# Attention with bucket masks, then two mixing layers: the score scale moves into the key split and the unmatched rows are mended behind the exponential

## The chip, the cores and the metric

One core of one Trainium2 chip runs the whole program. The metric is device time in microseconds (us). The kernel before took 697.1 us as the median of three runs (696.8 to 697.82).

## The reference, cut to what matters

For each of 2 x 8 heads, with 768 positions of 64 values, a row of scores may only see the keys whose bucket (six sign bits of a projection) is its own:

```python
scores = scale * np.matmul(q, k.transpose(0, 1, 3, 2))        # scale = 1/8
scores = np.where(mask, scores, -1000000000.0)
scores = scores - np.max(scores, axis=-1, keepdims=True)
attn = np.exp(scores)
attn = attn / (np.sum(attn, axis=-1, keepdims=True) + 1e-09)
return np.matmul(attn, v).astype(np.float32)
```

A row that matches no key has -1e9 everywhere, so its attention is even, 1/768 for each key. The result goes through a layer with cosines, sines and a token mixing, and then through a layer norm and an MLP of width 2048, each with residuals.

## The kernel before, in words

float32 accuracy is reached with pairs of fp32r tiles: each operand is split into a high part (`split_hi`, a cast on ScalarE, ACT) and a low part (`split_lo`, raw value minus high part, on VectorE, DVE, or GpSimd, POOL). The mask is added inside the score matmul: extra rows of bits lower an unmatched score by multiples of 2^34, so that an unmatched entry is hugely negative.

The attention works through 48 periods p. A period takes two tiles, a and b, of 128 rows by 768 keys. Its operations are named in the plans (L405 to L425): `Sa`/`Sb` score matmuls on TensorE (PE) into one PSUM tile each (one buffer per letter), `Ma`/`Mb` the negated row maximum on DVE (`s_max`, L288), `ta`/`tb` two operations on 128x1 on POOL (`s_tiny`, L292 and L293), `Ea`/`Eb` the exponential on ACT with its row sum (`s_exp`, L300), `R1` the sum plus 1e-9 (`s_guard`: DVE for p below 3, L308, POOL for the other 45, L310), `R2` the reciprocal on DVE (`s_recip`, L314), `na`/`nb` the normalization on POOL (`s_norm`, L318), `U0..U2` transposes on PE (L331), `H0..H2` their high parts on ACT (L340), `L0..L2` their low parts on DVE (L101), `PV` the product with v on PE (L356), `O` on ACT and `X` on DVE its evacuation (L365, L372).

In `s_tiny`, POOL makes two things from the negated maximum m: the scale, 0.125 if m is under 2^33 and 0 if not, and the bias, m times that scale. A row without a match so gets exp(0) = 1 everywhere, and its sum is 768.

The order on each engine in the attention is written out by hand: a step k goes through a plan and emits each operation for period k minus its lag. `plan_s` is for the first four steps, `plan_b` where bits of the later heads are computed, `plan` for the rest. `G`, `C` and `D` are places for background work: splits of q, k and v for later heads, the conversion of the theta weights (DVE: L121 and L124 in `D`, between `R1` and `R2`). In the plan, POOL's order in a step is `nb`, `G`, `R1`, `ta`, `na`, `C`, `tb`; DVE's is `Ma`, `X`, `D`, `R2`, `Mb`, `L0`, `L1`, `L2`. Engines work in the order of their own queue, so an operation that waits holds up what is behind it. Before step 1, PE runs 38 spare transposes (`warm`, L441). The last three steps and all that follows (the mixing layers) are put in order by a planner, not by hand.

The low parts of k are made on DVE for the head pairs 0, 2 and 3, and on POOL for pair 1 (whole, 128x768) and for pairs 4 to 7 (in two halves of 128x384 each).

Of the kernel before, what the change touches and what calls it, by code (L numbers as in the profile page):

```python
# [9 lines left out]
F32 = mybir.dt.float32  # L10
F32R = mybir.dt.float32r
U32 = mybir.dt.uint32
AF = mybir.ActivationFunctionType
ALU = mybir.AluOpType
AX = mybir.AxisListType
# [11 lines left out]
MISS = 2.0 ** 34  # L27
# [6 lines left out]
def attn_moe_kernel(  # L34
# [17 lines left out]
    B, H, D, S = qT.shape  # L52
# [11 lines left out]
    def f(ap):  # L64
        return ap.bitcast(F32)
# [26 lines left out]
    def cast(eng, o, i):  # L92
        if eng is act:
            act.activation(o, i, AF.Copy)  # L94
        elif eng is vec:
            vec.tensor_copy(o, i)
        else:
            pool.tensor_scalar(out=o, in0=i, scalar1=1.0, scalar2=0.0, op0=ALU.mult, op1=ALU.add)

    def sub(eng, o, i, hi):  # L100
        eng.tensor_tensor(out=o, in0=i, in1=f(hi), op=ALU.subtract)  # L101
# [64 lines left out]
    def split_hi(nm, n, eng, part=None):  # L166
        if part in (None, 0):
            hl[nm, n, 0] = bp.tile([128, S], F32R, tag=f"hi{nm}{n % NP}", name=f"hi{nm}{n}")
        r = part_of(S, part)
        cast(eng, hl[nm, n, 0][:, r], raw[nm, n][:, r])  # L170

    def split_lo(nm, n, eng, part=None):
        if part in (None, 0):
            hl[nm, n, 1] = bp.tile([128, S], F32R, tag=f"lo{nm}{n % NP}", name=f"lo{nm}{n}")
        r = part_of(S, part)
        sub(eng, hl[nm, n, 1][:, r], raw[nm, n][:, r], hl[nm, n, 0][:, r])

    vv_t = {}

# [104 lines left out]
        s_ps[p, i] = ps  # L284

    def s_max(p, i):
        m = ap_.tile([128, 3], F32, tag="m", bufs=4, name=f"m{p}_{i}")
        vec.tensor_reduce(out=m[:, 0:1], in_=s_ps[p, i][:, :, 0:HALF], axis=AX.XY, op=ALU.max, negate=True)  # L288
        m_t[p, i] = m
    def s_tiny(p, i):  # L290
        m = m_t[p, i]
        pool.tensor_scalar(out=m[:, 1:2], in0=m[:, 0:1], scalar1=MISS / 2, scalar2=0.125, op0=ALU.is_lt, op1=ALU.mult)  # L292
        pool.tensor_tensor(out=m[:, 2:3], in0=m[:, 0:1], in1=m[:, 1:2], op=ALU.mult)  # L293

    def s_exp(p, i):
        ps, m = s_ps.pop((p, i)), m_t.pop((p, i))
        if i == 0:
            l_t[p] = ap_.tile([128, 2, 2], F32, tag="l", bufs=4, name=f"l{p}")
        pt = ap_.tile([128, 2, HALF], F32, tag=f"p{i}", bufs=2, name=f"p{p}_{i}")
        act.activation(  # L300
            pt, ps[:, :, 0:HALF], AF.Exp, bias=m[:, 2:3], scale=m[:, 1:2], accum_out=l_t[p][:, 0, i:i + 1]
        )
        p_t[p, i] = pt

    def s_guard(p):
        l = l_t[p]
        if p < 3:
            vec.tensor_scalar(out=l[:, 0, :], in0=l[:, 0, :], scalar1=1e-9, scalar2=None, op0=ALU.add)  # L308
        else:
            pool.tensor_scalar(out=l[:, 0, :], in0=l[:, 0, :], scalar1=1e-9, scalar2=0.0, op0=ALU.add, op1=ALU.add)  # L310

    def s_recip(p):
        l = l_t[p]
# [2 lines left out]
    def s_norm(p, i):  # L316
        pn = ap_.tile([128, NI, 128], F32, tag=f"pn{i}", bufs=2, name=f"pn{p}_{i}")
        pool.tensor_scalar(  # L318
            out=pn.rearrange("p c s -> p (c s)"), in0=p_t.pop((p, i)).rearrange("p c s -> p (c s)"),
            scalar1=l_t[p][:, 1, i:i + 1], scalar2=0.0, op0=ALU.mult, op1=ALU.add,  # L320
        )
        pn_t[p, i] = pn

# [285 lines left out]
    def run_bg(q):  # L609
# [5 lines left out]
    ops = {  # L615
        "Sa": lambda p: s_mm(p, 0), "Sb": lambda p: s_mm(p, 1),
        "Ma": lambda p: s_max(p, 0), "Mb": lambda p: s_max(p, 1),
        "ta": lambda p: s_tiny(p, 0), "tb": lambda p: s_tiny(p, 1),
        "Ea": lambda p: s_exp(p, 0), "Eb": lambda p: s_exp(p, 1),
        "R1": s_guard, "R2": s_recip, "na": lambda p: s_norm(p, 0), "nb": lambda p: s_norm(p, 1),  # L620
        "B1": lambda p: bits_chunk(*bq[p], "T1"), "B2": lambda p: bits_y_(*bq[p]),
# [447 lines left out]
```

## Time and profile before

| what | before |
|---|---|
| runs, median of three | 697.1 us |
| profiled execution, its span from first to last instruction | 694.3 us |
| PE busy over the span | 680.1 us (98%) |
| DVE busy | 479.2 us (69%) |
| ACT busy | 386.9 us (56%) |
| POOL busy | 297.7 us (43%) |

The page of the profile gives no other time of the profiled execution than its span; the median of the runs lies 2.8 us above it. A busy PE is one with a matmul in flight, which says nothing of how closely the matmuls follow each other. The attention takes the first 240 us or so, and there all five engines are busy; in the rest of the span PE alone is.

### The profile page before, as it was taken

The page shows a single profiled execution, that of the slowest core. Times are in us where ns is not written, and L with a number is a line of the kernel's source. Part 1 is how long each engine was busy: PE and PEld are TensorE (multiplying, and loading weights), DVE is VectorE, ACT ScalarE, POOL GpSimd, SP SyncE. Part 2 cuts the span into 40 slices and gives each one's busy share as a digit, 9 for nine tenths or more (in the row PEclk, how much of TensorE's full clock was granted, in tenths as well). Part 3 has the DMA queues.
Part 4 walks back from the last instruction along what each step waited for, and adds up shares of the span by engine and source line. Part 5 has one row for each costly group of instructions (what it writes and reads, how often), then busy time and mean ns, then how long its engine had stood idle before and what let it go on. Part 6 is the DMA issues. An engine that isn't in the chain of part 4 may idle for free.

```text
span 694.3 us, 10787 instructions
## 1 busy us (share of the span) xinstructions
PE 680.1 (98%) x3694; PEld 583.3 (84%) x3694; DVE 479.2 (69%) x815; ACT 386.9 (56%) x757; POOL 297.7 (43%) x534
## 2 busy tenths in 40 slices
PE   9899999999999989999999999999999999999997
PEld 7799999999899868877888888888888888888885
DVE  6799998999999998897698789433655741121212
ACT  6799998999999976675454455211424421111110
POOL 5888889787878843334367613200121200000000
PEclk9999999999999999999999999999999999999999
DMA  8695554375552231111363335100112200010101
GB/s 256 155 200 157 145 119 107 92 166 139 124 134 77 77 91 46 47 45 46 96 185 100 121 111 190 63 1 1 62 60 79 105 1 0 1 61 0 61 0 61
DMA packets 30394, 62.17 MB, mean 90 GB/s; under 512 B 4274, under 2 KB 11058, under 8 KB 30340
## 3 DMA queue, kind: packets, MB, share of 16 engines
q1 hardware_dynamic: 30340, 61.48, 31.6%
q8 instruction: 30, 0.49, 0.3%
q14 instruction: 24, 0.20, 0.1%
HBM read 39.98 MB, written 3.15 MB: 62 GB/s over the span
## 4 chain that ended last, share of the span: by engine, by line
PE 53%; DVE 20%; ACT 10%; POOL 7%; issue 6%; DMA 2%; SPq 1%; POOLq 0%; ACTq 0%; DVEq 0%
PE h L947 19%; PE oc L966 19%; DVE m L288 3%; DVE ptl L101 3%; ACT p L300 3%; PE s L280 3%; PE o L356 3%; PE a L798 3%; PE t L331 3%; DVE cs L121 2%; ACT pth L340 2%; DVE cy L124 2%; PE acc L757 2%; DVE z L101 2%; POOL pn L318 2%
## 5 line engine op out<-in xcount | busy, mean ns | idle before, releaser
L117 POOL TENSOR_SCALAR cs<-st 128x256 f32<-128x256 f32 (+2 forms) x78 | 52.1, 672 | 154.3 <-DVE cy L124 84.5
L950 ACT ACTIVATE hh<-h 128x512 fp32r<-128x512 f32 x48 | 28.5, 596 | 143.7 <-PE h L947 109.6
L300 ACT ACTIVATE p<-s,m 128x768 f32<-128x768 f32 x96 | 95.5, 995 | 7.2 <-POOL m L293 5.6
L951 DVE SCALAR_TENSOR_TENSOR hl<-h,hh 128x512 fp32r<-128x512 f32 x48 | 32.8, 685 | 93.8 <-ACT hh L950 93.8
L288 DVE TENSOR_REDUCE m<-s 128x1 f32<-128x768 f32 x96 | 90.8, 947 | 8.0 <-PE s L280 4.1
L757 PE MATMUL acc<-z,tokh 128*128 128x512 f32 x288 | 91.2, 395 | 1.1 <-ACT z L94 0.4
L318 POOL TENSOR_SCALAR pn<-p,l 128x768 f32<-128x768 f32 x96 | 87.5, 912 | 10.7 <-DVE l L314 8.7
L101 DVE TENSOR_TENSOR ptl<-t,pth 128x512 fp32r<-128x512 f32 x144 | 91.1, 680 | 0.3 <-ACT pth L340 0.2
L280 PE MATMUL s<-tk,tq 128*128 128x384 f32 (+1 forms) x360 | 82.1, 350 | 2.1 <-ACT p L300 1.9
L331 PE MATMUL t<-ident,pn 128*128 128x128 f32 x576 | 81.1, 274 | 1.7 <-POOL pn L318 1.2
L340 ACT ACTIVATE pth<-t 128x512 fp32r<-128x512 f32 x144 | 81.1, 595 | 1.5 <-PE t L331 0.2
L331 PEld LDWEIGHTS t<-ident,pn 128*128 128x128 f32 x576 | 67.7, 140 | 9.2 <-POOL pn L318 1.7
L966 PE MATMUL oc<-w2h,hh 128*128 128x512 f32 x192 | 75.0, 391 | 0.3 <-ACT hh L950 0.2
L966 PE MATMUL oc<-w2l,hh 128*128 128x512 f32 x192 | 74.9, 390 | 0.0
L966 PE MATMUL oc<-w2h,hl 128*128 128x512 f32 x192 | 74.7, 391 | 0.0
L757 PEld LDWEIGHTS acc<-z,tokh 128*128 128x128 f32 x288 | 53.3, 188 | 13.2 <-DVE z L101 1.3
L280 PEld LDWEIGHTS s<-tk,tq 128*128 128x128 f32 (+1 forms) x360 | 58.5, 189 | 6.9 <-ACT p L300 6.6
L114 ACT ACTIVATE cy<-st 128x256 f32<-128x256 f32 (+2 forms) x78 | 42.7, 552 | 31.2 <-DVE w2l L101 8.4
L121 DVE SCALAR_TENSOR_TENSOR cs<-st,cs 128x256 uint32<-128x256 uint32 (+2 forms) x78 | 54.3, 699 | 5.9 <-POOL cs L117 5.7
L757 PE MATMUL acc<-z,tokl 128*128 128x512 f32 x144 | 55.5, 391 | 0.0
L124 DVE SCALAR_TENSOR_TENSOR cy<-cy,cs 128x256 uint32<-128x256 uint32 (+2 forms) x78 | 48.3, 627 | 3.0 <-ACT cy L114 2.2
L356 PE MATMUL o<-pth,vv 128*128 128x256 f32 x288 | 46.5, 296 | 0.2 <-POOL vv L101 0.2
(174 smaller groups left out, 1402.7 us busy)
## 6 DMA issues: line engine op xcount, KB each, us to landing
st<-in_w_dram SPq DMA_DIRECT2D x26, 512.0 KB
tq<-hiq SPq DMA_DIRECT2D x30, 192.0 KB
tk<-hik SPq DMA_DIRECT2D x30, 192.0 KB
st<-in_wrT_dram SPq DMA_DIRECT2D x12, 384.0 KB
st<-in_wiT_dram SPq DMA_DIRECT2D x12, 384.0 KB
vs<-in_v_dram SPq DMA_DIRECT2D x8, 384.0 KB
st<-in_w_dram SPq DMA_DIRECT2D x12, 256.0 KB
out_dram<-U SPq DMA_DIRECT2D x12, 256.0 KB
```

The costliest lines, as they stand in the source:

```text
L101: eng.tensor_tensor(out=o, in0=i, in1=f(hi), op=ALU.subtract)
L121: vec.scalar_tensor_tensor(out=su, in0=t[:, :, 0], scalar=29, in1=su, op0=ALU.logical_shift_right, op1=ALU.bitwise_or)
L280: pe.matmul(ps[:, hf, 0:HALF], lt[0:K, x * 128:(x + 1) * 128], rt[0:K, hf * HALF:(hf + 1) * HALF], start=(K == 128), stop=(K != 128),)
L288: vec.tensor_reduce(out=m[:, 0:1], in_=s_ps[p, i][:, :, 0:HALF], axis=AX.XY, op=ALU.max, negate=True)
L300: act.activation(pt, ps[:, :, 0:HALF], AF.Exp, bias=m[:, 2:3], scale=m[:, 1:2], accum_out=l_t[p][:, 0, i:i + 1])
L318: pool.tensor_scalar(out=pn.rearrange("p c s -> p (c s)"), in0=p_t.pop((p, i)).rearrange("p c s -> p (c s)"), scalar1=l_t[p][:, 1, i:i + 1 ...
L331: pe.transpose(ps[:, w * 128:(w + 1) * 128], pn_t[p, i][:, c, :], ident)
L340: act.activation(ph, t_ps[p, u], AF.Copy)
L356: pe.matmul(ps, vv[:, c, e].rearrange("p a d -> p (a d)"), x[:, c::NI, :], start=(k == 0), stop=(k == 2 * NI - 1),)
L757: pe.matmul(acc, w[:, x, t * 128:(t + 1) * 128], z[:, x, y, :], start=(j == 0 and k == 0), stop=(j == NI - 1 and k == 5),)
L947: pe.matmul(ps, w[:, d, x * 128:(x + 1) * 128], XN[k][y][:, d, :], start=(n == 0), stop=(n == 11))
L966: pe.matmul(acc2[t], lt[:, t * 128:(t + 1) * 128], w[:, x, :], start=(first and n == 0), stop=(last and n == 2),)
```

## The change

k is multiplied by 1/8 at its split: the high part by the scale of the cast; the low part on DVE in one operation with two inputs (k times 0.125 minus the high part), on POOL by an extra operation in place on the raw tile before the subtraction. The exponential then takes the negated maximum itself as bias and no scale, so `s_tiny` goes. In its place `s_lone` runs once a period at the place of `tb`, on 128x2 for both tiles: two POOL operations that give 1/768 and 1e30 where m is at least 2^33 (no match), else 0. `R1` adds 1e-9 and the second of these to the sum, now on DVE for every period, and `s_norm` adds the first to the normalized row. A row without a match so gets something divided by about 1e30, plus 1/768. The tile m is one of 128x3x2 for each period where it was one of 128x3 for each letter; four buffers both times.

```diff
-        cast(eng, hl[nm, n, 0][:, r], raw[nm, n][:, r])
+        eng.activation(hl[nm, n, 0][:, r], raw[nm, n][:, r], AF.Copy, scale=0.125 if nm == "k" else 1.0)
...
-        sub(eng, hl[nm, n, 1][:, r], raw[nm, n][:, r], hl[nm, n, 0][:, r])
+        hi, lo = (hl[nm, n, y][:, r] for y in range(2))
+        x = raw[nm, n][:, r]
+        if nm == "q":
+            sub(eng, lo, x, hi)
+        elif eng is vec:
+            vec.scalar_tensor_tensor(out=lo, in0=x, scalar=0.125, in1=f(hi), op0=ALU.mult, op1=ALU.subtract)
+        else:
+            pool.tensor_scalar(out=x, in0=x, scalar1=0.125, scalar2=0.0, op0=ALU.mult, op1=ALU.add)
+            sub(pool, lo, x, hi)
...
     def s_max(p, i):
-        m = ap_.tile([128, 3], F32, tag="m", bufs=4, name=f"m{p}_{i}")
-        vec.tensor_reduce(out=m[:, 0:1], in_=s_ps[p, i][:, :, 0:HALF], axis=AX.XY, op=ALU.max, negate=True)
-        m_t[p, i] = m
-    def s_tiny(p, i):
-        m = m_t[p, i]
-        pool.tensor_scalar(out=m[:, 1:2], in0=m[:, 0:1], scalar1=MISS / 2, scalar2=0.125, op0=ALU.is_lt, op1=ALU.mult)
-        pool.tensor_tensor(out=m[:, 2:3], in0=m[:, 0:1], in1=m[:, 1:2], op=ALU.mult)
+        if i == 0:
+            m_t[p] = ap_.tile([128, 3, 2], F32, tag="m", bufs=4, name=f"m{p}")
+        vec.tensor_reduce(
+            out=m_t[p][:, 0, i:i + 1], in_=s_ps[p, i][:, :, 0:HALF], axis=AX.XY, op=ALU.max, negate=True
+        )
+
+    def s_lone(p):
+
+        m = m_t[p]
+        for x, c in ((1, 1.0 / S), (2, 1e30)):
+            pool.tensor_scalar(
+                out=m[:, x, :], in0=m[:, 0, :], scalar1=MISS / 2, scalar2=c, op0=ALU.is_ge, op1=ALU.mult
+            )
...
-            pt, ps[:, :, 0:HALF], AF.Exp, bias=m[:, 2:3], scale=m[:, 1:2], accum_out=l_t[p][:, 0, i:i + 1]
+            pt, ps[:, :, 0:HALF], AF.Exp, bias=m[:, 0, i:i + 1], accum_out=l_t[p][:, 0, i:i + 1]
...
     def s_guard(p):
         l = l_t[p]
-        if p < 3:
-            vec.tensor_scalar(out=l[:, 0, :], in0=l[:, 0, :], scalar1=1e-9, scalar2=None, op0=ALU.add)
-        else:
-            pool.tensor_scalar(out=l[:, 0, :], in0=l[:, 0, :], scalar1=1e-9, scalar2=0.0, op0=ALU.add, op1=ALU.add)
+        vec.scalar_tensor_tensor(
+            out=l[:, 0, :], in0=l[:, 0, :], scalar=1e-9, in1=m_t[p][:, 2, :], op0=ALU.add, op1=ALU.add
+        )
...
-            scalar1=l_t[p][:, 1, i:i + 1], scalar2=0.0, op0=ALU.mult, op1=ALU.add,
+            scalar1=l_t[p][:, 1, i:i + 1], scalar2=m_t[p][:, 1, i:i + 1], op0=ALU.mult, op1=ALU.add,
...
-        "ta": lambda p: s_tiny(p, 0), "tb": lambda p: s_tiny(p, 1),
+        "ta": lambda p: None, "tb": s_lone,
```

## Rows read from the trace of the kernel before

**Rows 1.** Busy time by engine in windows: start:end, length, then engines, granted clock.

```profile
40.00:80.00 40.00, 39.61 (x297) 37.70 (x296) 38.02 (x65) 39.10 (x82) 36.25 (x75) 1.00 0.61 148
...
200.00:240.00 40.00, 39.50 (x283) 36.07 (x281) 38.93 (x72) 38.88 (x81) 31.86 (x69) 1.00 0.26 85
240.00:280.00 40.00, 36.87 (x188) 30.21 (x187) 37.42 (x62) 29.52 (x55) 17.18 (x19) 1.00 0.23 68
...
440.00:480.00 40.00, 40.00 (x192) 33.06 (x191) 13.76 (x23) 7.59 (x13) 2.72 (x4) 1.00 0.00 0
```

**Rows 2.** Waits by engine, steady attention (40 to 250 us): total, times, longest.

```profile
PEld s L280 <- ACT p L300: 6.3, 20, 0.7
...
ACT p L300 <- POOL m L293: 1.4, 3, 0.7
```

**Rows 3.** Groups of instructions, shapes apart: count, busy and mean, idle before.

```profile
L318 POOL TENSOR_SCALAR pn<-p,l 128x768 f32<-128x768 f32 x96 | 87.5, 912 | 10.7 <-DVE l L314 8.7 <-PE t L331 0.7 <-PE s L280 0.3
...
L292 POOL TENSOR_SCALAR m<-m 128x1 f32<-128x1 f32 x96 | 23.8, 248 | 12.9 <-DVE m L288 7.8 <-DVE l L308 1.9
...
L293 POOL TENSOR_TENSOR m<-m 128x1 f32<-128x1 f32 x96 | 19.1, 199 | 7.9
...
L310 POOL TENSOR_SCALAR l<-l 128x2 f32<-128x2 f32 x45 | 11.0, 243 | 7.4 <-ACT p L300 4.5
```

**Rows 4.** Timeline of DVE, 17 us: the guard and reciprocal of period 0.

```profile
17.45 0.16 DVE L308 TENSOR_SCALAR l<-l 128x2 f32<-128x2 f32 x1
17.65 0.17 DVE L314 RECIPROCAL l<-l 128x2 f32<-128x2 f32 x1
```

**Rows 5.** Timeline of all engines, 10 to 20 us: start, duration, instruction.

```profile
10.01 1.81 POOL L101 TENSOR_TENSOR lok<-rawk,hik 128x768 fp32r<-128x768 f32 x1
10.02 2.03 DVE L101 TENSOR_TENSOR pb_hi<-pbr,pb_hi 128x192 fp32r<-128x192 f32 x1 [0.20 <-ACT pb_hi L94]
...
10.52 4.37 PE L441 MATMUL warm<-ident 128*128 128x128 f32 x38
...
15.55 0.65 POOL L467 TENSOR_SCALAR bits<-bb,cst_sb 64x384 fp32r<-64x384 f32 x1
...
15.60 0.99 ACT L300 ACTIVATE p<-s,m 128x768 f32<-128x768 f32 x1 [0.96 <-POOL m L293]
...
15.93 0.61 PE L459 MATMUL s<-bk,bits 7*128 7x384 f32 x2
...
16.73 0.62 PE L451 MATMUL s<-tkz,hiq 128*128 128x384 f32 x2 [0.19 <-ACT p L300]
```

**Rows 6.** Timeline of ACT and PE, 29 to 30 us.

```profile
29.07 0.99 ACT L300 ACTIVATE p<-s,m 128x768 f32<-128x768 f32 x1 [2.22 <-POOL m L293]
...
29.97 0.44 PE L331 MATMUL t<-ident,pn 128*128 128x128 f32 x2 [1.22 <-POOL pn L318]
```

**Rows 7.** Timeline of POOL, DVE and ACT, 138 to 140 us.

```profile
137.99 0.73 POOL L101 TENSOR_TENSOR thl<-cy,thh 128x256 fp32r<-128x256 f32 x1
...
138.18 0.42 DVE L372 TENSOR_TENSOR xT<-o,ot 64x256 f32<-64x256 f32 x1
...
139.08 0.17 DVE L314 RECIPROCAL l<-l 128x2 f32<-128x2 f32 x1 [0.48 <-POOL l L310]
...
139.67 0.99 ACT L300 ACTIVATE p<-s,m 128x768 f32<-128x768 f32 x1 [0.69 <-POOL m L293]
```

**Rows 8.** Busy time over one cycle of six periods, 160.58 to 187.38 us.

```profile
sum 26.80, PE 26.43 PEld 24.52 DVE 25.79 ACT 26.17 POOL 21.18; mean PE 8.81 PEld 8.17 DVE 8.60 ACT 8.72 POOL 7.06
```

**Rows 9.** Timeline of that cycle's turn, 182 to 188 us.

```profile
182.78 0.24 POOL L310 TENSOR_SCALAR l<-l 128x2 f32<-128x2 f32 x1
...
187.38 0.42 DVE L372 TENSOR_TENSOR xT<-o,ot 64x256 f32<-64x256 f32 x1 [0.57 <-ACT ot L365]
```

**Rows 10.** Timeline of the last period's b, 232 to 236 us.

```profile
232.44 0.93 DVE L288 TENSOR_REDUCE m<-s 128x1 f32<-128x768 f32 x1
...
236.04 1.03 ACT L300 ACTIVATE p<-s,m 128x768 f32<-128x768 f32 x1
```

More of the change, by code (lines that the diff above doesn't have):

```diff
@@ L286, in s_max @@
     def s_max(p, i):
-        m = ap_.tile([128, 3], F32, tag="m", bufs=4, name=f"m{p}_{i}")
-        vec.tensor_reduce(out=m[:, 0:1], in_=s_ps[p, i][:, :, 0:HALF], axis=AX.XY, op=ALU.max, negate=True)
-        m_t[p, i] = m
-    def s_tiny(p, i):
-        m = m_t[p, i]
-        pool.tensor_scalar(out=m[:, 1:2], in0=m[:, 0:1], scalar1=MISS / 2, scalar2=0.125, op0=ALU.is_lt, op1=ALU.mult)
-        pool.tensor_tensor(out=m[:, 2:3], in0=m[:, 0:1], in1=m[:, 1:2], op=ALU.mult)
+        if i == 0:
[9 more added lines that the diff above has]
+            )
     def s_exp(p, i):
-        ps, m = s_ps.pop((p, i)), m_t.pop((p, i))
+        ps, m = s_ps.pop((p, i)), m_t[p]
         if i == 0:
```

## The prediction, made before the changed kernel ran

> **What bounds the kernel now.** I read the busy times by window first. From 440 us on PE is busy 40.00 of 40 us and the other engines mostly idle; in 40 to 80 and 200 to 240 us PE, DVE and ACT are each busy over 38 of 40 [rows 1]. So the late part can't gain, and whatever the attention wins or loses reaches the end one for one, since PE has no slack behind it in which to lose it again. The change touches only the attention (the first 240 us) and what leaves it.
>
> Then the waits. In the steady attention the two small POOL operations hold the exponential up for 1.4 us in all, three times, and PE's score matmuls wait 6.3 us for an exponential to free their PSUM tile [rows 2]. So the delay that the change removes is mostly hidden: the exponential comes when ACT's own queue lets it. The timelines show where it isn't hidden: the first four steps [rows 5, 6], one place at 139 us [rows 7], and the drain of the last period [rows 10]. Last I read the stretch with the theta conversions, which repeats a cycle of six periods in 26.80 us: DVE is busy 25.79, ACT 26.17, PE 26.43 of it [rows 8]. What is to be seen there is that no engine has much room, DVE 1.01 us per cycle.
>
> **The change, part by part.** POOL loses 96 times 248 and 199 ns and 45 times 243 ns, 23.8 + 19.1 + 11.0 = 53.9 us [rows 3]. It gains two operations per period on 128x2, 96 in all; the nearest are the 243 and 248 ns of the same rows, so about 23.8 us. The scaling of k on POOL adds one 128x768 operation and eight of half that size: 912 ns for a whole one [rows 3], a half between 456 and 912, so 4.6 to 8.2 us. POOL is relieved by 53.9 - 23.8 - 4.6 (or 8.2) = 22 to 25.5 us; it is the engine with the most idle time in the attention (31.86 of 40 busy [rows 1]), so this counts only through waits. Behind each added scaling wait the subtraction and then `na`; its cover is POOL's idle time, and without it each would delay the transposes by its 0.5 to 0.9 us. Scaling in the cast adds no instruction to ACT; the low part of k on DVE keeps its two inputs and its size, so I cost both at nothing, at most 0.05 us for each DVE split, at a time when DVE waits for PE anyway.
>
> DVE gains 45 guards. When guard and reciprocal stood on DVE before, they started at 17.45 and 17.65: 0.20 us, since the second needs the first [rows 4]. That is the price with `R2` right behind; with a conversion between them it is between nothing and 0.20, I take 0.10. In a theta cycle four guards are of the first kind and two of the second: 4 x 0.20 + 2 x 0.10 = 1.0 us, as much as DVE's whole idle time there, 26.80 - 25.79 = 1.01 [rows 8]. Over the cycle's long DVE part the lag builds up, and behind it come `Mb`, the exponential and the low parts. It meets 0.57 us in which `X` waits for ACT [rows 9] and some 0.4 in smaller pieces. On the other side the exponential starts some 0.5 us sooner after the maximum (248 + 199 ns and the steps between), so DVE may be that much later without ACT noticing, and ACT's own idle time is 0.63 us per cycle. The bounds for the cycle are +1.0 (nothing is absorbed) and -0.37 (PE's idle time, 26.80 - 26.43, is the most that can be won). I take 0, for the 3.5 cycles of that stretch too; their bounds are +3.5 and -1.3. In the rest of the steady attention, as from 40 to 80 us, DVE is idle 40 - 38.02 = 1.98 us [rows 1], over some nine periods (4.4 us each) about 0.2 us per period, which is the guard's price; I take 0 there as well.
>
> The start. Exponential b of period 0 waited 0.96 us for POOL, and the scores of period 1 that need its PSUM tile left PE idle 0.19 us [rows 5]. PE's spare transposes run from 10.52 to 14.89, so nothing before that can help. Between 0.19 (what PE shows) and 0.96 (the whole wait) I take 0.4, two such waits, one for each letter. At 29.07 the exponential waited 2.22 us for POOL, but PE's next stop, 1.22 us, is for a normalized tile [rows 6], behind which POOL does as many operations as before; I take 0, bounds 0 and -1.2. At 10.01 a low part of k on POOL and a small split on DVE start together; DVE's took 2.03, to the end of POOL's 1.81 [rows 5]. The scaling now stands ahead of that subtraction: the DVE split either slips in between (sooner, covered by the spare transposes) or ends behind both (up to 0.9 later, 0.4 after what the exponential gains). I take 0, bound +0.4.
>
> At 139 us the reciprocal waited 0.48 for a guard that stood behind POOL's conversion, and the exponential 0.69 [rows 7]. The guard on DVE goes right behind `X`, from 138.60; with 0.20 the reciprocal starts at 138.80 and not at 139.08: -0.3, bounds 0 and -0.7.
>
> The drain. The last maximum ended at 233.37, its exponential started at 236.04 [rows 10], 2.67 us later, as POOL had two normalizations (2 x 0.9 us) and weight conversions ahead of `tb`. ACT could be there some 1.8 us sooner, but DVE is busy 37.42 of 40 us right behind and PE loses only 40 - 36.87 = 3.1 us there [rows 1]. A third of 1.8: -0.6, bounds 0 and -1.8.
>
> Sum: -0.4 - 0.3 - 0.6 = -1.3 us. On the profiled execution 694.3 becomes 693.0; the median lies 2.8 above the span, so 695.8. 0.2% is 1.4 us, about what a measurement of this kernel can tell from no change.
>
> **The rivals.**
>
> *DVE becomes the bound of the theta stretch (slower).* If of the 1.01 us only the 0.57 at `X` can be used, and all six guards cost 0.20, the cycle grows by 1.2 - 0.57 = 0.63, and 3.5 cycles by 2.2: with the gains elsewhere 695.8 + 2.2 = 698.0; with nothing absorbed 699.3. It decides against the gains from 1.3 / 3.5 = 0.37 per cycle, that is from a guard of (0.57 + 0.37) / 6 = 0.16 us. For it speaks that DVE is full there; against it that each period's later maximum has half a microsecond of new room before ACT misses it. A second way to a dear guard: at 10.02 a DVE operation with both inputs in SBUF stood still until POOL's was over [rows 5], and the new guard also reads two SBUF tiles. But POOL's guard started at 182.78, so by then POOL was through with its background work, and its next long operation waits for the reciprocal: the port is mostly free when DVE's guard comes. The Trainium skill (SBUF — State Buffer, Who interferes with whom) states this as a lock: a DVE instruction with two SBUF inputs and a GpSimd one that reads SBUF exclude each other, the later is blocked for the whole instruction, while a DVE instruction with at most one SBUF input, outside the two-port modes, is free of it. The trace agrees at 10.02; by that rule a guard that meets a normalization waits up to 912 ns where the old one-input form would not, and 45 half waits would be some 20 us, an upper estimate that the order of the queues excludes.
>
> *The waits pay in full (faster).* The start gives 0.96 and the 1.22 of PE, 139 us gives 0.69, with the drain's 0.6: 3.5 us, 693.6. For it: POOL's relief moves everything that stands behind it. Against it: PE's queue is in order and at the start holds bit matmuls and transposes that wait for POOL's same number of operations.
>
> *The planner orders the drain and the mixing otherwise.* It sees other durations on POOL and DVE. PE loses 3.1 us in 240 to 280; half of that either way is 694.3 or 697.4, with the other terms.
>
> *Letter a waits for b.* The maxima of both letters now lie in one tile; were waits kept by whole tiles, `Ea` would wait for `Mb`. The trace excludes it: at 15.93 PE read one half of the bits tile while POOL wrote the other until 16.20 [rows 5].
>
> **How the numbers follow.** The forecast (a small gain, 694.7 to 696.8) gets 0.50, about half of it over 0.2%: faster 0.26, same 0.24. DVE as bound 0.24: slower 0.18, same 0.06. Full waits 0.18, all faster. The planner 0.08: 0.03, 0.02, 0.03. Faster 0.47, same 0.32, slower 0.21. The range reaches into both rivals, from 693.2, below the full waits, to 698.8, between the DVE rival's two times.
>
> **What would show it.** Right: the exponential's waits for POOL gone; the reciprocal at most 0.2 us behind the guard on DVE; a theta cycle of 26.6 to 27.0 us; the stop of 0.48 at 139 us gone; the last exponential at its maximum's end. Wrong: cycles of 27.2 us and more with DVE without idle time, guards on DVE longer than 0.2 us while POOL is busy, or another order of work behind 234 us that moves PE's idle time there.

## The result and the profile after

The changed kernel takes 703.35 us (median of four runs, 702.47 to 704.25) against 697.33 for the kernel before, measured beside it: a ratio of 1.0087, 95% interval 1.0073 to 1.0101. It is 6 us slower, where a small gain was forecast. The profiled span grew from 694.3 to 700.7 us, and by where the time lies the 6.4 us split into parts. The marks are the starts of letter a's maximum in period 4 (the steady attention begins), in period 46 (the drain begins), and the last `xT`; each was read in the timeline of DVE.

| stretch | before | after |
|---|---|---|
| start to the maximum of period 4 | 35.51 | 35.16 |
| periods 4 to 46 | 190.95 | 194.37 |
| maximum of period 46 to the last `xT` | 31.00 | 33.20 |
| last `xT` to the end | 436.9 | 438.0 |

The attention loses 3.4 us and the part behind it 3.3. The windows of the changed kernel (columns as in [rows 1]) show both:

```profile
40.00:80.00 40.00, 39.11 (x293) 36.47 (x290) 39.44 (x73) 37.40 (x80) 32.25 (x49) 1.00 0.58 144
200.00:240.00 40.00, 39.03 (x291) 35.95 (x289) 39.50 (x80) 37.59 (x82) 27.89 (x45) 1.00 0.26 85
240.00:280.00 40.00, 34.76 (x177) 28.13 (x178) 37.53 (x60) 28.35 (x54) 19.26 (x21) 1.00 0.23 69
440.00:480.00 40.00, 40.00 (x189) 33.06 (x189) 17.29 (x34) 7.98 (x14) 4.72 (x7) 1.00 0.09 30
```

POOL and ACT are less busy from 40 to 80 us than in [rows 1], yet PE is too, and DVE has gone from 38.02 to 39.44 of 40 (an instruction that stands still counts as busy): the bound has moved to DVE. From 240 to 280 PE is busy 34.76 in place of 36.87.

The groups of the changed operations (count, busy, mean ns, idle before), to be held against [rows 3]:

```profile
L332 POOL TENSOR_SCALAR pn<-p,l,m 128x768 f32<-128x768 f32 x96 | 95.7, 998 | 49.1 <-DVE l L328 28.6 <-ACT p L315 8.4 <-PE t L345 5.8
...
L315 ACT ACTIVATE p<-s,m 128x768 f32<-128x768 f32 x96 | 86.8, 905 | 1.5 <-DVE m L298 0.5 <-DVE l L322 0.5
...
L306 POOL TENSOR_SCALAR m<-m 128x2 f32<-128x2 f32 x96 | 23.7, 247 | 5.9 <-DVE m L298 0.6
...
L322 DVE SCALAR_TENSOR_TENSOR l<-l,m 128x2 f32<-128x2 f32 x48 | 15.2, 317 | 0.7
...
L184 POOL TENSOR_SCALAR rawk<-rawk 128x384 f32<-128x384 f32 x8 | 4.1, 514 | 0.6
```

The line that stands out is the guard on DVE: 128x2 like the 0.16 us of [rows 4], but 317 ns on average, where its neighbour, the reciprocal, takes 162. A mean of twice the shortest says that some instructions are far longer. The timeline of DVE and POOL around one of them:

```profile
84.57 0.51 POOL L184 TENSOR_SCALAR rawk<-rawk 128x384 f32<-128x384 f32 x1
85.17 1.00 POOL L101 TENSOR_TENSOR lok<-rawk,hik 128x384 fp32r<-128x384 f32 x1
85.19 0.42 DVE L386 TENSOR_TENSOR xT<-o,ot 64x256 f32<-64x256 f32 x1
85.64 0.55 DVE L322 SCALAR_TENSOR_TENSOR l<-l,m 128x2 f32<-128x2 f32 x1
86.22 0.17 DVE L328 RECIPROCAL l<-l 128x2 f32<-128x2 f32 x1
86.31 0.94 DVE L298 TENSOR_REDUCE m<-s 128x1 f32<-128x768 f32 x1
86.57 0.99 POOL L332 TENSOR_SCALAR pn<-p,l,m 128x768 f32<-128x768 f32 x1 [0.40 <-DVE l L328]
```

The guard starts at 85.64, nothing is ahead of it, and it ends at 86.19, just behind the end of POOL's subtraction (85.17 + 1.00 = 86.17). Fifteen of the 48 guards took 0.33 to 0.92 us, twelve of them to the end of a subtraction that POOL was in, three to that of another POOL operation; the others took 0.14 to 0.18. The twelve that were held in periods 5 to 25 stand 6.8 us longer in all than 0.15 each would. In the kernel before, the subtraction of this step was over well before `X` ended, so that a guard behind `X` would have met nothing:

```profile
83.18 1.01 POOL L101 TENSOR_TENSOR lok<-rawk,hik 128x384 fp32r<-128x384 f32 x1
84.51 0.42 DVE L372 TENSOR_TENSOR xT<-o,ot 64x256 f32<-64x256 f32 x1
```

There the subtraction starts 1.33 us ahead of `X`, in the changed kernel 0.02. POOL, done at 86.17, then waits another 0.40 for the reciprocal that had to come behind the guard. The view of waits from 40 to 250 us shows who is late (total, times, longest):

```profile
POOL pn L332 <- DVE l L328: 26.0, 30, 2.3
PEld t L345 <- POOL pn L332: 10.8, 27, 0.6
ACT pth L354 <- PE t L345: 9.2, 26, 0.7
...
ACT p L315 <- DVE m L298: 0.5, 2, 0.3
```

The exponential's waits for POOL [rows 2] are gone as forecast; in their place POOL waits for DVE (8.7 us, 15 times before), the transposes for POOL, and ACT for the transposes (0.2 us before). These totals are not the loss: with the guard as a reduction (below), where the attention is faster than in the kernel before, the first three are still 21.1, 7.6 and 6.2 us.

In the drain PE's stops are other ones than before. Its timeline (the bracket is the idle time before and what ended it):

```profile
246.77 0.98 PE L370 MATMUL o<-pth,vv 128*128 128x256 f32 x6 [1.04 <-DVE xT L386]
...
249.40 1.25 PE L730 MATMUL xps<-ident,xT 128*128 128x128 f32 x8 [0.82 <-DVE ptl L101]
...
251.01 0.50 PE L736 MATMUL xth<-thh,xh 128*128 128x512 f32 x1 [0.36 <-ACT U L731]
...
253.00 0.50 PE L736 MATMUL xth<-thh,xl 128*128 128x512 f32 x1 [0.77 <-DVE xl L101]
...
268.69 1.30 PE L771 MATMUL acc<-z,tokh 128*128 128x512 f32 x3 [2.17 <-ACT z L94]
```

The same view of the same stretch in the kernel before:

```profile
244.45 0.66 PE L716 MATMUL xps<-ident,xT 128*128 128x128 f32 x4 [0.52 <-DVE ptl L101]
246.13 0.50 PE L722 MATMUL xth<-thh,xh 128*128 128x512 f32 x1 [1.02 <-ACT U L717]
254.85 0.50 PE L722 MATMUL th<-thh,xh 128*128 128x512 f32 x1 [1.12 <-ACT U L717]
258.66 0.50 PE L757 MATMUL acc<-z,tokh 128*128 128x512 f32 x1 [0.33 <-DVE z L101]
```

These are 5.16 and 2.99 us of stops. The planned orders of PE and ACT are the same in both kernels up to the drain and differ from there. The wait that the drain's forecast was made of did shrink: the last exponential starts 0.72 us behind its maximum's end, in place of 2.67.

### The profile page after: what moved, and what is told of

It reads as the page before. It is cut to its first block, busy times and chain, and to the rows that moved or that the text cites. A ratio compares the mean times of both kernels' runs of the same rounds, so it can differ in the third digit from the quotient of the medians.

```text
span 700.7 us, 10694 instructions
## 1 busy us (share of the span) xinstructions
PE 680.9 (97%) x3694; PEld 581.3 (83%) x3694; DVE 490.3 (70%) x860; ACT 379.2 (54%) x757; POOL 284.1 (41%) x402
## 4 chain that ended last, share of the span: by engine, by line
PE 45%; DVE 26%; ACT 5%; issue 4%; POOL 3%; DMA 1%; ACTq 0%; POOLq 0%; DVEq 0%
PE h L961 19%; PE oc L980 19%; DVE ptl L101 6%; DVE m L298 6%; PE a L812 3%; PE acc L771 2%; DVE z L101 2%; DVE cy L124 2%; DVE cs L121 2%; DVE xT L386 1%; POOL cs L117 1%; DVE r L741 1%; DVE kk L748 1%; ACT t L744 1%; ACT kk L745 1%
## 5 line engine op out<-in xcount | busy, mean ns | idle before, releaser
L332 POOL TENSOR_SCALAR pn<-p,l,m 128x768 f32<-128x768 f32 x96 | 95.7, 998 | 49.1 <-DVE l L328 28.6
L345 PE MATMUL t<-ident,pn 128*128 128x128 f32 x576 | 87.5, 277 | 7.5 <-POOL pn L332 5.8
L354 ACT ACTIVATE pth<-t 128x512 fp32r<-128x512 f32 x144 | 83.9, 598 | 11.4 <-PE t L345 9.2
L315 ACT ACTIVATE p<-s,m 128x768 f32<-128x768 f32 x96 | 86.8, 905 | 1.5 <-DVE m L298 0.5
```

Of the source, the lines that this page charges most:

```text
L315: act.activation(pt, ps[:, :, 0:HALF], AF.Exp, bias=m[:, 0, i:i + 1], accum_out=l_t[p][:, 0, i:i + 1])
L332: pool.tensor_scalar(out=pn.rearrange("p c s -> p (c s)"), in0=p_t.pop((p, i)).rearrange("p c s -> p (c s)"), scalar1=l_t[p][:, 1, i:i + 1 ...
L345: pe.transpose(ps[:, w * 128:(w + 1) * 128], pn_t[p, i][:, c, :], ident)
L354: act.activation(ph, t_ps[p, u], AF.Copy)
```

## The experiments

Two losses had to be explained, the attention's and the drain's. The theory for the first: the guard on DVE is held by a POOL operation, and the scaling of k is what pushes POOL's subtraction under the guard. Rivals: POOL's added time by itself, or the normalization's longer form. For the second: the planner's order. The rival: DVE comes into the drain later and fuller.

All runs, in stretches as above ("held": guards of more than 0.3 us on DVE). The medians of the runs before were 698.23, 697.23, 697.06 and 696.47 us in the four groups. From 40 to 226 us every profiled execution shows a granted clock of 1.00, so periods 4 to 46 compare alike. Elsewhere the mean of some windows lies below it: 0.91 from 0 to 40 us in the reduction without scaling (its period 4 began at 40.14 us), 0.96 there in three others, 0.95 from 226 to 260 us in the guard on POOL, the mask on POOL and the reduction with two guards on POOL, 0.98 from 260 to 340 us in five.

| run | time | ratio, 95% interval | periods 4 to 46 | 46 to last `xT` | held |
|---|---|---|---|---|---|
| before | | 1 | 190.95 | 31.00 | 0 |
| changed | 703.35 | 1.0087 [1.0073, 1.0101] | 194.37 | 33.20 | 15 |
| no scaling of k on POOL | 701.29 | 1.0036 [1.0010, 1.0062] | 190.39 | 33.20 | 7 |
| guard on POOL | 700.26 | 1.0036 [1.0012, 1.0061] | 192.51 | 30.54 | 2 |
| one-input guard | 703.97 | 1.0069 [1.0038, 1.0099] | 194.59 | 33.20 | 15 |
| scale from a tile | 704.19 | 1.0075 [1.0037, 1.0112] | 194.53 | 33.18 | 15 |
| guard as a reduction | 697.97 | 1.0002 [0.9986, 1.0018] | 188.76 | 33.15 | 0 |
| scaling on ACT | 700.65 | 1.0047 [1.0032, 1.0063] | 192.22 | 33.19 | 7 |
| reduction, scaling on ACT | 700.15 | 1.0025 [1.0004, 1.0046] | 190.95 | 33.19 | 0 |
| reduction, no scaling | 697.96 | 1.0008 [0.9997, 1.0019] | 188.26 | 33.74 | 0 |
| reduction, scale from a tile | 700.03 | 1.0037 [1.0018, 1.0056] | 189.87 | 33.16 | 0 |
| no guard, mask on POOL | 700.03 | 1.0043 [1.0029, 1.0058] | 189.34 | 33.98 | 0 |
| before, last guard on DVE | 699.47 | 1.0034 [1.0010, 1.0058] | 191.02 | 32.38 | 0 |
| reduction, last two guards on POOL | 696.92 | 0.9992 [0.9978, 1.0006] | 188.82 | 30.61 | 0 |
| changed, old tail | 698.73 | 1.0038 [1.0024, 1.0052] | 194.17 | 30.97 | 14 |
| reduction, old tail | 694.18 | 0.9962 [0.9949, 0.9974] | 188.79 | 30.97 | 0 |

### The attention

**No scaling of k on POOL.**

```diff
-            pool.tensor_scalar(out=x, in0=x, scalar1=0.125, scalar2=0.0, op0=ALU.mult, op1=ALU.add)
```

> The changed kernel without POOL's extra scaling of k (the low parts of k for head pairs 1 and 4 to 7 are made from the unscaled raw tile, so their scores are scaled wrongly). PE's and ACT's order of work is that of the changed kernel. Theory 1, the lock: twelve of the two-input guards stood 0.48 to 0.92 us until a POOL subtraction ended, eight of them under a subtraction of k that the scaling had pushed back by 0.5 us; without the scaling those are free, and the last period's first maximum starts 2.0 to 3.0 us sooner than 234.31, the whole run 2 to 3 us sooner than 703.4. Theory 2, the guard's own 0.2 us on a full DVE: the periods stay at 4.35 us, at most 0.5 us sooner.

The attention is 4.0 us shorter, and 7 guards are held in place of 15; of the seven that lay under a subtraction of k (the expectation counts eight) none is. The timeline of POOL and DVE at the same step as above:

```profile
84.64 1.01 POOL L101 TENSOR_TENSOR lok<-rawk,hik 128x384 fp32r<-128x384 f32 x1
85.44 0.42 DVE L385 TENSOR_TENSOR xT<-o,ot 64x256 f32<-64x256 f32 x1
85.89 0.16 DVE L321 SCALAR_TENSOR_TENSOR l<-l,m 128x2 f32<-128x2 f32 x1
```

The subtraction, with no scaling ahead of it, starts 0.80 us ahead of `X`, is over at 85.65, and the guard at 85.89 takes 0.16. The scaling costs by what it puts under the guard.

**Guard on POOL.**

```diff
-        vec.scalar_tensor_tensor(
-            out=l[:, 0, :], in0=l[:, 0, :], scalar=1e-9, in1=m_t[p][:, 2, :], op0=ALU.add, op1=ALU.add
-        )
+        (vec if p < 3 else pool).tensor_tensor(out=l[:, 0, :], in0=l[:, 0, :], in1=m_t[p][:, 2, :], op=ALU.add)
```

> The changed kernel with the guard back on POOL from period 3 on (one addition of two 128x2 tiles; the 1e-9 is left out, which is nothing beside a sum of at least 1). Both theories of the guard, lock and own price, expect the attention back: the last period's first maximum at 230.5 to 231.5 us. If the slower normalization (998 for 912 ns) or later normalized tiles are the cause, it stays above 233. The planner orders the drain anew here, so what comes after that maximum may differ by some 2 us either way.

Periods 4 to 46 are 1.9 us shorter, still 1.6 over the kernel before: from period 3 on no guard is on DVE to be held, but it stands in POOL's queue behind scaling and subtraction, and DVE's reciprocal waits for it 9.0 us in 13 waits from 40 to 250 us, where it waited 0.9 in 3 in the kernel before. The last period's first maximum, at 232.80, falls between the two theories' times. The planner also ordered the drain otherwise.

**One-input guard.** The mend of unmatched rows in the sum is left out, to see whether the second input is what gets held.

```diff
-            out=l[:, 0, :], in0=l[:, 0, :], scalar=1e-9, in1=m_t[p][:, 2, :], op0=ALU.add, op1=ALU.add
+            out=l[:, 0, :], in0=l[:, 0, :], scalar1=1e-9, scalar2=None, op0=ALU.add
```

> The changed kernel with a one-input guard on DVE (1e-9 added, the mending of unmatched rows in the sum left out). PE's and ACT's order is that of the changed kernel. Theory 1, the lock: no guard is over 0.2 us, and the last period's first maximum starts 3 to 4 us sooner than 234.31, at 230.3 to 231.3, the run at 699.4 to 700.4. Theory 2, its own price: all guards still take 0.2 us of DVE; less than 1 us sooner.

A miss: 194.59, no gain. The timeline shows why; the guard with one input is held too, to the end of the subtraction:

```profile
90.37 1.00 POOL L101 TENSOR_TENSOR lok<-rawk,hik 128x384 fp32r<-128x384 f32 x1
90.61 0.79 DVE L322 TENSOR_SCALAR l<-l 128x2 f32<-128x2 f32 x1
91.43 0.17 DVE L326 RECIPROCAL l<-l 128x2 f32<-128x2 f32 x1
```

So "two inputs" is too narrow a statement of what is held. A row of the kernel before speaks of another form: a reciprocal, one input too, ran through a POOL subtraction untouched.

```profile
108.73 1.98 POOL L101 TENSOR_TENSOR loq<-rawq,hiq 128x384 fp32r<-128x384 f32 x2
108.84 0.15 DVE L314 RECIPROCAL l<-l 128x2 f32<-128x2 f32 x1
```

The Trainium skill (SBUF — State Buffer, Who interferes with whom) sorts the forms in this way: a tensor_scalar can use both ports and then contends with GpSimd, an instruction with two SBUF inputs contends with a GpSimd instruction that reads SBUF, a reduction on trn2 never does. This case's rows agree with the first two (0.79 and 0.55 us); the run with the guard as a reduction tests the third.

**Scale from a tile.** The exponential had become shorter without anyone's forecast; does that hide part of the loss?

```diff
-            pt, ps[:, :, 0:HALF], AF.Exp, bias=m[:, 0, i:i + 1], accum_out=l_t[p][:, 0, i:i + 1]
+            pt, ps[:, :, 0:HALF], AF.Exp, bias=m[:, 0, i:i + 1], scale=ones, accum_out=l_t[p][:, 0, i:i + 1]
```

> The changed kernel with the exponential's scale read from a tile of ones, as a tile was read before: 995 ns instead of 905. Order of work as in the changed kernel. If the shorter exponential (96 x 0.09 = 8.6 us of ACT) hides part of the loss, 1 to 4 us slower than 703.4, above all in periods 9 to 18 and in the theta stretch, where ACT was the bound before; if DVE alone bounds, within 0.5 us of it.

194.53 (the exponential takes 996 ns): with the guard held, its 90 ns change nothing that shows in the attention.

**Guard as a reduction.** The value that marks a lone row is written beside the row sums, and DVE adds the two columns (the 1e-9 is left out).

```diff
...
-        vec.scalar_tensor_tensor(
-            out=l[:, 0, :], in0=l[:, 0, :], scalar=1e-9, in1=m_t[p][:, 2, :], op0=ALU.add, op1=ALU.add
-        )
+        vec.tensor_reduce(
+            out=l[:, 3, :], in_=l[:, 0:3:2, :].rearrange("p x i -> p i x"), axis=AX.X, op=ALU.add
+        )
...
```

> The guard on DVE becomes a sum over two columns (a reduction: one input, a row sum and beside it the value that marks a lone row) in place of a scalar_tensor_tensor of two tiles; the same number of instructions, the same order on PE and ACT, POOL keeps its scaling of k. Theory 1 (a held guard): a guard with two inputs, or a tensor_scalar with one, stands still until POOL's running subtraction ends, while a DVE reduction does not; then no guard takes over 0.25 us and periods 4 to 46 take 191 to 193 us, 1.5 to 3.5 less than the changed kernel's 194.4. Theory 2 (POOL itself is late: scaling and subtraction stand ahead of the normalization, and the guard's wait is only seen on the way): the guards may be short, yet periods 4 to 46 stay at 194 to 195, since the normalization can't start before the subtraction ends. Drain (maximum of period 46 to the last xT) 33.2 as in the changed kernel by both, as the order of PE is the same.

188.76: 5.6 us below the changed kernel, more than theory 1 asked, and 2.2 below the kernel before. POOL still has its scaling, and the subtraction still lies over the guard; it just isn't held:

```profile
87.59 1.00 POOL L101 TENSOR_TENSOR lok<-rawk,hik 128x384 fp32r<-128x384 f32 x1
87.84 0.14 DVE L321 TENSOR_REDUCE l<-l 128x2 f32<-128x4 f32 x1
88.02 0.17 DVE L327 RECIPROCAL l<-l 128x2 f32<-128x2 f32 x1
88.58 0.99 POOL L331 TENSOR_SCALAR pn<-p,l,m 128x768 f32<-128x768 f32 x1
```

POOL goes from the subtraction to the normalization without a stop, where it had waited 0.40. All 48 take 0.13 to 0.16 us, seventeen of them wholly inside an operation of POOL, which agrees with the third statement above. Same order on PE and ACT, same number of instructions, one changed form: this is the attention's cause, and theory 2 falls. The normalization takes 993 ns here too, so its longer form isn't the loss either.

**Scaling on ACT, and both.** For the pairs whose low part POOL makes, ACT scales raw k in place ahead of the cast.

```diff
-        eng.activation(hl[nm, n, 0][:, r], raw[nm, n][:, r], AF.Copy, scale=0.125 if nm == "k" else 1.0)
+        x, c = raw[nm, n][:, r], 0.125 if nm == "k" else 1.0
+        if nm == "k" and n in (1, 4, 5, 6, 7):
+            act.activation(x, x, AF.Copy, scale=0.125)
+            c = 1.0
+        eng.activation(hl[nm, n, 0][:, r], x, AF.Copy, scale=c)
...
-            pool.tensor_scalar(out=x, in0=x, scalar1=0.125, scalar2=0.0, op0=ALU.mult, op1=ALU.add)
```

> The scaling of raw k by 1/8 moves from POOL to ACT for the pairs whose low part POOL makes (one whole tile and eight halves, in place, ahead of the cast); POOL has its old subtraction alone, ACT 8 more instructions of 0.4 to 0.6 us. If POOL's scaling is what lengthened the attention, by whichever way, periods 4 to 46 take 190.4 (what leaving it out gave) to 192 (ACT was busy too, but now stops less), against the changed kernel's 194.4. If ACT is the bound of those periods, each of them grows by up to 0.5 and the sum is 193 to 195. The drain stays 33.2 us.

> Both: the guard as a reduction and the scaling of k on ACT. Theory 1: no guard and no scaling is in anyone's way, periods 4 to 46 at 189.5 to 190.9, below the kernel before (190.95); with the changed kernel's drain (33.2) and late part the time is 698 to 700. Theory 2: the same as with the scaling on ACT alone.

ACT has eight more instructions, two on whole tiles and six on halves. 192.22 and 190.95, each a little above its range: 1.8 us above leaving the scaling out, and 2.2 above the reduction alone. In the attention these instructions cost more on ACT than on POOL; and without the reduction seven guards are still held.

**Reduction, no scaling.** Unlike the first experiment, this asks what the scaling costs once no guard can be held (same edit, on the reduction).

> The guard as a reduction, and POOL's scaling of k left out (the low parts of k then have the wrong scale). Theory 1 (the scaling costs only by what it puts under a guard): with no guard held, leaving it out gives nothing, periods 4 to 46 at 188.3 to 188.8 against 188.76 with the reduction alone. Theory 2 (POOL's own time counts): 187 or less, some 0.2 us for each of nine scalings. Drain 33.2.

188.26: 0.5 us for all nine. POOL's idle time does cover the scaling; what it did not cover was where the subtraction went. With the first experiment the four cases are complete: 188.26 with neither the scaling nor the two-input guard, 188.76 with the scaling alone, 190.39 with the guard alone, 194.37 with both. Alone they cost 0.5 and 2.1 us, together 6.1.

**Reduction, scale from a tile.** (The edit of the fourth experiment, on the reduction.)

> The guard as a reduction, and the exponential again with its scale read from a tile (all ones), 995 ns in place of 905. With the reduction the attention is 2.2 us shorter than in the kernel before; if the shorter exponential is where that comes from, it goes here: periods 4 to 46 at 190.5 to 191. If the exponential's 90 ns are covered, as where the guard was held, 188.8, and the gain comes from POOL's missing small operations.

189.87, between the two: the shorter exponential is worth 1.1 of the 2.2 us by which the attention beats the kernel before. The other 1.1 is left for the missing small operations and the mended place at 139 us; no run takes these alone.

**No guard, mask on POOL.** Of `s_lone`'s two values the second is here 1 for a row with a match and 0 for one without.

```diff
...
     def s_guard(p):
-        l = l_t[p]
-        vec.scalar_tensor_tensor(
-            out=l[:, 0, :], in0=l[:, 0, :], scalar=1e-9, in1=m_t[p][:, 2, :], op0=ALU.add, op1=ALU.add
-        )
+        pass
...
+        if i == 0:
+            l = l_t[p]
+            pool.tensor_tensor(out=l[:, 1, :], in0=l[:, 1, :], in1=m_t[p][:, 2, :], op=ALU.mult)
```

> No guard at all: DVE takes the reciprocal of the raw sum, and POOL multiplies it by 0 or 1 (one operation of 128x2, some 0.25 us) just ahead of the first normalization; the output is the reference's. The reciprocal is one input and was never held in any run. DVE has 45 instructions less than with the reduction (0.1 to 0.2 us each), POOL one more between reciprocal and normalization. Periods 4 to 46 at 188 to 189.5 (a gain on DVE against 0.25 us on the way to the transposes). The planner orders the drain otherwise again: 30.5 to 33.2.

189.34 in the attention, as expected, and the longest drain of all, 33.98, above what was expected (its window from 226 to 260 us at a granted clock of 0.95): a better attention is lost again behind it.

### The drain

**The kernel before, with its last guard on DVE.**

```diff
-        if p < 3:
+        if p < 3 or p == 47:
```

> The kernel before with one edit: only the guard of the last period goes from POOL to DVE. It leaves the attention as it is, but the planner orders the drain and the mixing otherwise from there. Theory (the drain's loss is the order's, not the work's): periods 4 to 46 stay at 190.9 to 191.2, and the time from the maximum of period 46 to the last xT is more than 0.5 us off the 31.0 of the kernel before, and the rest after it more than 0.5 off too, one way or the other. If the drain's loss in the changed kernel comes from the guard on DVE itself (0.5 us held, conversions ahead of X), it shows here as well, at 31.5 to 33.2; if it comes from neither, 31.0.

The attention is untouched (191.02), that one guard is not held, and the drain is 1.4 us longer, and from its end to the last instruction of an engine it takes 434.89 us in place of 433.69: 2.6 us in all. The guard ends at 238.07, where POOL's ended at 237.53. The reciprocal follows at 239.39 (237.82 before), behind other work of DVE, and the normalization comes 2.6 us later, behind two more operations on the weights in POOL's order. In the kernel before:

```profile
238.51 2.09 POOL L318 TENSOR_SCALAR pn<-p,l 128x768 f32<-128x768 f32 x2
```

With the last guard on DVE:

```profile
237.90 0.17 DVE L308 TENSOR_SCALAR l<-l 128x2 f32<-128x2 f32 x1
...
241.15 2.47 POOL L318 TENSOR_SCALAR pn<-p,l 128x768 f32<-128x768 f32 x2
...
242.10 0.87 PE L331 MATMUL t<-ident,pn 128*128 128x128 f32 x6 [1.01 <-POOL pn L318]
```

One instruction on another engine is enough for the planner to order the drain otherwise, and the time follows.

**Reduction, last two guards on POOL.**

On top of the reduction:

```diff
...
+        if p >= 46:
+            pool.tensor_tensor(out=l[:, 3, :], in0=l[:, 0, :], in1=l[:, 2, :], op=ALU.add)
+            return
...
```

> The guard as a reduction on DVE, and on POOL (one addition) for the last two periods, where POOL has no low parts left; that alone makes the planner order the drain as in the run with all guards on POOL (30.5 us from the maximum of period 46 to the last xT). Periods 4 to 46 as with the reduction alone, 188.8 (bounds 188.5 to 189.2), maximum to xT 30.5. If the order sets the drain's length, the drain is 2.6 us shorter than with the reduction alone; but in the run with all guards on POOL PE stood 1.9 us longer between 330 and 440 us, so of the 2.6 only 0.5 to 1 may reach the end: 696 to 697.5. If the drain is long for another reason (more work on DVE), it stays at 33 us here.

The drain is 2.5 us shorter than with the reduction alone, though PE stands 2.85 us in it, up to 244.94, and the granted clock falls behind that stop (mean of 245 to 250 us: 0.66). Behind it PE stands another 1.35 us at 329.38, and from the last `xT` to the last instruction of an engine it takes 436.71 us: 696.92, as expected, and not to be told from the kernel before.

**The old tail, on the changed kernel and on the reduction.** For periods 45 to 47 the small operations have the form of the kernel before. That gives PE and ACT exactly its planned order.

```diff
...
+        old = dict(bias=m[:, 2, i:i + 1], scale=m[:, 1, i:i + 1]) if p >= 45 else dict(bias=m[:, 0, i:i + 1])
+        act.activation(pt, ps[:, :, 0:HALF], AF.Exp, accum_out=l_t[p][:, 0, i:i + 1], **old)
...
+        if p >= 45:
+            pool.tensor_scalar(out=l[:, 0, :], in0=l[:, 0, :], scalar1=1e-9, scalar2=0.0, op0=ALU.add, op1=ALU.add)
+            return
...
-            scalar1=l_t[p][:, 1, i:i + 1], scalar2=m_t[p][:, 1, i:i + 1], op0=ALU.mult, op1=ALU.add,
+            scalar1=l_t[p][:, 1, i:i + 1], scalar2=0.0 if p >= 45 else m_t[p][:, 1, i:i + 1], op0=ALU.mult, op1=ALU.add,
...
-        "ta": lambda p: None, "tb": s_lone,
+        "ta": lambda p: s_tiny(p, 0) if p >= 45 else None,
+        "tb": lambda p: s_tiny(p, 1) if p >= 45 else s_lone(p),
```

> The changed kernel with its two-input guard, and the old small operations for the last three periods alone; PE and ACT again in exactly the planned order of the kernel before. Theory (the order makes the drain's loss): periods 4 to 46 at 194.2 to 194.5 as in the changed kernel, the drain back at 31.0, PE standing 5.3 us behind it, the time 2.5 to 3.5 us below the changed kernel: 700 to 701. Rival (the drain is long because DVE comes into it later and fuller): 33 us, 703.

> The guard as a reduction, and for the last three periods the small operations of the kernel before (two on POOL per letter, scale from a tile, guard on POOL); with that the planned order of PE and ACT is exactly that of the kernel before. If the account is complete (held guards for the attention, the planned order for the drain), periods 4 to 46 take 188.8 to 189.0, the maximum of period 46 to the last xT 31.0, PE stands 5.3 us from there to the end, and the time is 2 us below the kernel before: 694.5 to 695.5. If the drain's loss has another cause, the drain stays at 32 to 33 and the time at 697 or more.

With the changed kernel's attention (194.17) the drain is back at 30.97, though DVE comes into it 3 us later than before: the rival that put the loss down to that falls. The last exponential is back at 2.68 us behind its maximum's end, so the wait that the forecast wanted to remove is not what sets the drain's length. The time, 698.73, is below the range expected; by the two ratios this run lies 3.4 us under the changed kernel. One window each, from the maximum of period 46 to the last instruction of an engine, of the kernel before,

```profile
226.46:691.16 464.70, 459.40 (x2134) 378.67 (x2131) 274.73 (x463) 176.41 (x330) 114.38 (x148) 1.00 0.20 63
```

the changed kernel,

```profile
229.53:697.83 468.30, 460.38 (x2133) 378.42 (x2131) 276.77 (x466) 175.16 (x328) 114.80 (x142) 1.00 0.19 62
```

and the changed kernel with the old tail:

```profile
229.43:694.09 464.66, 459.43 (x2133) 378.61 (x2131) 274.66 (x463) 176.40 (x330) 114.50 (x149) 1.00 0.20 63
```

464.70, 468.30, 464.66 us: 3.6 us more under the new order, of which PE stands 468.30 - 460.38 = 7.92 in place of 5.30 and is busy 1.0 longer; nothing of it is left under the old order. One execution each is too little for the size. Eight other runs have the changed kernel's order on PE; the three of them whose granted clock is 1.00 throughout behind 226 us (scale from a tile, scaling on ACT, reduction without scaling) take 467.4 to 468.3 us here, with 7.6 to 7.8 of stops, and the third run with the old order (the reduction below) 465.25, with 5.4. So the order costs 2 to 4 us: 2.1 to 2.7 in stops, the rest in PE's busy time, which differs by 0.7 between runs of one order. This run gives back the old work of three periods along with the old order; that the order by itself costs is shown by the single moved guard, 2.6 us.

The reduction with the old tail has both causes gone. It takes 694.18 us, a little below the range expected, ratio 0.9962 [0.9949, 0.9974]: 0.4% under the kernel before. The same stops of PE as before, under the same order:

```profile
242.37 0.66 PE L737 MATMUL xps<-ident,xT 128*128 128x128 f32 x4 [0.53 <-DVE ptl L101]
244.04 0.50 PE L743 MATMUL xth<-thh,xh 128*128 128x512 f32 x1 [1.02 <-ACT U L738]
252.77 0.50 PE L743 MATMUL th<-thh,xh 128*128 128x512 f32 x1 [1.13 <-ACT U L738]
256.57 0.50 PE L778 MATMUL acc<-z,tokh 128*128 128x512 f32 x1 [0.34 <-DVE z L101]
```

## Why the prediction was wrong

**The step that failed first** is the guard's price on DVE, 0.20 us "with `R2` right behind", and the sentence that dropped the dear guard: "the port is mostly free when DVE's guard comes". It was free for 33 of the 48 guards; the loss is in the others. The second way to a dear guard was on the page, with the row that shows the mechanism [rows 5]. It was set aside by one row from the theta stretch [rows 9], and carried over to periods 4 to 22, where POOL makes the low parts of k and q. From the maximum of period 4 to that of period 22 the changed kernel takes 85.97 us in place of 82.34, from there to period 46 108.41 in place of 108.61: the whole loss of the attention is in the first part. Fifteen held guards of 0.33 to 0.92 us are what the runs showed in place of that price; without them the attention is 5.6 us shorter. The upper estimate of 20 us counted half a normalization for every guard, and the order of the queues did keep these away, as the prediction said: one guard of 48 met one (period 2, 0.76 us). What it left out were the subtractions, which twelve met. The same passage took the old one-input form to be free; the one-input run shows it held (0.79 us).

**The scaling of k** was costed at nothing, with POOL's idle time as cover. As POOL time this was right (0.5 us for nine, with the reduction). But it was weighed only for what waits behind it on POOL. It also moved the subtraction onto the guard, from 0.80 us ahead of `X` to 0.02: 4.0 us, with the two-input guard in place. Two edits, each harmless by the working, made most of the loss together (6.1 us against 0.5 and 2.1 alone).

**The stop at 139 us**, forecast at -0.3, is not gone but has moved into the guard. It is the same step of period 25, under the same subtraction of the theta weights:

```profile
141.44 0.73 POOL L101 TENSOR_TENSOR thl<-cy,thh 128x256 fp32r<-128x256 f32 x1
...
141.71 0.48 DVE L322 SCALAR_TENSOR_TENSOR l<-l,m 128x2 f32<-128x2 f32 x1
142.22 0.17 DVE L328 RECIPROCAL l<-l 128x2 f32<-128x2 f32 x1
```

`X` ended at 141.68, so the reciprocal starts 0.54 us behind it, where it was 0.48 in [rows 7]; with the reduction it is 0.22 (136.57 to 136.79). The forecast's 0.20 from guard to reciprocal failed here as in the rest.

**The drain**, forecast at -0.6, cost 3.6 us (2 to 4 by all runs). Its exponential came 1.95 us sooner behind its maximum, as the working had it, and no run shows anything won by that. The rival of the planner had the mechanism and the place; it was given 0.08 and half of 3.1 us either way, and both were too small. The bound taken, PE's idle time in the kernel before, limits a gain; a loss it does not limit. Nor does what the attention wins reach the end one for one: the 2.2 us of the reduction did not reach it under the new order (697.97 us against 697.23). Behind the attention PE is not alone in being busy: DVE is busy 37.42 of 40 us from 240 to 280 us [rows 1], and most of PE's stops there wait for DVE or ACT.

**The rest of the steady attention and the theta stretch**, forecast at 0: the theta cycle measures

```profile
sum 26.73, PE 26.16 PEld 24.23 DVE 26.34 ACT 25.05 POOL 18.63; mean PE 13.08 PEld 12.11 DVE 13.17 ACT 12.52 POOL 9.31
```

against 26.80 in [rows 8], as forecast, with DVE at 26.34 (0.39 idle, 1.01 before): the guards went into its idle time. The rival of DVE as the bound so fell where it was put. Without held guards the whole of periods 4 to 46 would have gained 2.2 us, which the prediction didn't have: it took the exponential and the normalization to keep their durations. They went from 995 to 905 and from 912 to 998 ns.

**Right** were the exponential's waits for POOL in the steady attention, which are gone, the theta cycle, and the sizes of the new POOL operations (247 ns; 4.1 + 0.8 us for the scaling). The start came out as forecast (-0.35 measured at period 4, -0.4 forecast), but that is not shown to be the forecast's mechanism: the three runs with the reduction that start alike reach period 4 at 35.27, 35.36 and 35.62 us, and in the changed kernel two guards are held on the way (0.33 and 0.76 us). POOL was relieved by 297.7 - 284.1 = 13.6 us and not 22 to 25.5, mostly for the normalization's 96 x 86 ns = 8.3. The lock of letter a to b didn't show. Full waits, worth 3.5 us, were never seen whole.

**The sum** with what was measured: -0.35 at the start, +5.6 held guards, -2.2 elsewhere in the attention, +3.6 in the drain and behind it = +6.65 to the last instruction of an engine, where the marks give 697.83 - 691.16 = 6.67; the span, which ends some 3 us behind that, has 6.4, the medians 6.0.

## What to carry to other kernels

Before a small operation goes to DVE, look at what POOL is in when it will start, stretch by stretch, and choose a form that isn't held: here a reduction in the place of a tensor_scalar or a two-input operation took 5.6 us off with PE and ACT in the same order of work. An operation that is covered on its own engine can still push another under a neighbour; follow the shifted one too. Where a planner orders what follows, count any edit near the border as a new draw, and test it by giving the new kernel the old order.

## What the runs showed of the hardware

A DVE tensor_scalar with one SBUF input (128x2) stands still until POOL's subtraction is over (0.79 us under one), as a two-input operation does (0.48 to 0.92); POOL's tensor_scalar holds them too (a two-input guard 0.76 us under a normalization). A reduction of 128x4 and a reciprocal of 128x2 run through a subtraction in 0.14 and 0.15.

An exponential on 128x768 takes 995 ns with its scale read from a tile and 905 with a constant one. The Trainium skill (ScalarE: Activation LUTs, What ACT_TABLE_LOAD costs) puts each such operand at about 93 ns; the rows agree, with 90. POOL's tensor_scalar on 128x768 went the other way, from 912 ns with a constant second scalar to 998 with one from a tile.
